# Hash products of a bucketed-attention and mixture-of-experts kernel: a second copy of queries and keys, half the columns, two diagonal blocks

## The chip, the cores and the metric

One core of one Trainium2 chip. The metric is the device time of one execution in microseconds (us); the number compared is the median of several executions of the same program.

## What is computed

Three stages follow each other; only the first is touched.

```python
q_bits = (np.einsum('bhsd,dk->bhsk', q, proj) > 0)      # 6 bits a token
k_bits = (np.einsum('bhsd,dk->bhsk', k, proj) > 0)
mask = q_bucket[:, :, :, None] == k_bucket[:, :, None, :]
scores = np.where(mask, scale * q @ k.T, -1e9)
attn = softmax(scores);  x = attn @ v                    # 2 x 8 heads, 768 tokens, 64 wide
x = moe(x)                                               # 8 experts, top 1, 512 -> 1024 -> 512
out = ((x @ w_a) * (x @ w_b)) @ w_out                    # 512 -> 1536 -> 512
```

All data are float32. The six signs of a token's product with `proj` (64 x 6) are its hash; a query sees the keys with the same hash.

## The kernel before

**Attention.** The 16 pairs of batch and head ("heads", h) run one after the other; a head has six tiles of 128 queries (t = 0 to 5), and the step counter g is 6h + t. The order of the instructions on each engine is written out by hand in the loop over g (from L740 on); waits between engines follow from the data. In step g, TensorE (PE) computes the scores of step g + 1 (`scores`, L160 and L161), then what stands in the list `early`, then the six transposes of the probabilities of step g (`tposes`, L188, two groups of three). VectorE (DVE) takes the smallest score of each row (L166) and a factor from it (L167), ScalarE (ACT) the exponential (L175). Each group of three transposes fills one of two PSUM buffers and is copied out by ACT (L192) or DVE (L194), as a table says; so the first group of a step can only be written when the copy of the first group of the step before has ended. In steps t = 1, 3 and 5 PE also multiplies the transposed probabilities of the head before with its values (`av_step`, L203), in t = 4 it makes the output of the head before that (`o_out`, L255).

**Inputs of a head.** `load` (L95) brings three DMAs on SyncE's (SP's) queue: X, queries in columns 0 to 767 and keys in 768 to 1535, where rows 64 to 127 repeat rows 0 to 63; and the values V. X has two buffers. `split_a` (L105, ACT) and `split_b` (L117 to L121, DVE and POOL) turn X into rounded parts T and remainders B of the head after next. The table `K` places them: for h > 1 the split of the queries by ACT (entry `sa`) stands in step t = 0 after the exponential.

**Hash.** `hash_mm` (L125) makes the products for head h + 1 in step t = 1 of head h (t = 0 of head 0). It is four float32 matmuls of 384 columns, two for the queries and two for the keys, each into 32 of PSUM's 128 rows (four column groups of the array). The stationary operand `pst` holds `proj`, its negative and zeros; its rows 64 to 127 are zero. `hash_codes` (L142) compares the whole block with thresholds in one DVE instruction (L144) and sends the 12 useful rows of each group by four DMAs (L149, SP's queue) into rows 64 to 75 of T. The first score matmuls of head h + 1, issued in step t = 5 of head h, read those rows (76 of 128 rows are active in L160). Head 0 takes `hash_code` (L137) instead.

**Other work on SP's queue in this stage.** 13 fills of a buffer in DRAM with zeros (L751) in heads 2 to 4, eight loads of expert weights (L506) that are issued in head 5, and in the end loads for the next stage. SP issues in order; an instruction that waits holds back everything behind it.

Of the kernel before, what the change touches and what calls it, by code (L numbers as in the profile page):

```python
# [7 lines left out]
F32 = mybir.dt.float32  # L8
F32R = mybir.dt.float32r
# [6 lines left out]
ALU = mybir.AluOpType  # L16
# [5 lines left out]
S, D, NB, NH = 768, 64, 2, 8  # L22
NT = 6
# [4 lines left out]
C_ID, C_TRI, C_THR, C_REV, C_TOK, C_IOTA, C_BASE, C_SLOT = 0, 128, 256, 258, 266, 278, 279, 287  # L28
# [6 lines left out]
def attn_moe_kernel(ctx: ExitStack, tc: tile.TileContext, xin, cst, projd, wblk, wmoe, w2in, out):  # L35
    nc = tc.nc
    PE, ACT, DVE, POOL = nc.tensor, nc.scalar, nc.vector, nc.gpsimd
# [14 lines left out]
    pst = big.tile([128, 64], F32, name="pst")  # L52
    thr = const.tile([128, 2], F32, name="thr")
# [25 lines left out]
    xp = ctx_a.enter_context(tc.tile_pool(name="xp", bufs=2))  # L79
# [4 lines left out]
    sm = ctx_a.enter_context(tc.tile_pool(name="sm", bufs=4))  # L84
# [3 lines left out]
    ps_m = ctx_a.enter_context(tc.tile_pool(name="ps_m", bufs=1, space=PSUM))  # L88

    NHD = NB * NH  # L90
    X, V, T, B, PT = {}, {}, {}, {}, {}
    st, pt_ = {}, {}
    scl, nbs, last = {}, {}, {}

    def load(h, first=()):  # L95
        X[h] = xp.tile([128, 2 * S], F32, tag="x", name="x")
        for i in range(2):
            after(nc.sync.dma_start(out=X[h][:, i * S:(i + 1) * S], in_=xin[h, :, i * S:(i + 1) * S]), first)
        V[h] = vp.tile([128, NT, D], F32, tag="v", name="v")
# [23 lines left out]
    hp_ = {}  # L123

    def hash_mm(h, order=range(4)):  # L125
        p = (ps_m if h or 2 in order else ps_a).tile([128, 512], F32, tag="m" if h or 2 in order else "a", name="m")
        for j in order:
            i = j // 2
            hp_[h, j] = p
            PE.matmul(  # L130
                p[32 * j:32 * j + 32, :384], pst[:, 32 * i:32 * i + 32], X[h][:, j * 384:(j + 1) * 384],
                start=True, stop=True, skip_group_check=True,
            )

    def hash_code(h, j):
        i, c = divmod(j, 2)
        DVE.tensor_scalar(  # L137
            out=T[h, i][64:76, c * 384:c * 384 + 384], in0=hp_[h, j][32 * j:32 * j + 12, :384],
            scalar1=thr[32 * j:32 * j + 12, 0:1], scalar2=(1.0, BIG)[i], op0=ALU.is_gt, op1=ALU.mult,
        )  # L140

    def hash_codes(h):  # L142
        c = sm.tile([128, 384], F32R, tag="code", name="code", bufs=1)
        DVE.tensor_scalar(  # L144
            out=c, in0=hp_[h, 0][:, :384], scalar1=thr[:, 0:1], scalar2=thr[:, 1:2], op0=ALU.is_gt, op1=ALU.mult
        )
        for j in range(4):
            i, k = divmod(j, 2)
            nc.sync.dma_start(  # L149
                out=T[h, i].bitcast(F32)[64:76, k * 384:k * 384 + 384], in_=c.bitcast(F32)[32 * j:32 * j + 12]  # L150
            )

    def scores(g):
        h, t = divmod(g, NT)
# [87 lines left out]
    def o_out(h, q=None):  # L242
        b, hh = divmod(h, NH)
        o, r = oT.pop((h, q)), rs.pop((h, q))
        p = ps_m.tile([128, 512], F32, tag="m", name="m")
        t0, nt = q or (0, NT)
        t = slice(b * 6 + t0, b * 6 + t0 + nt)
        lp = sm.tile([128, nt, 16], F32, tag=f"lp{nt}", name="lp", bufs=2) if hh else lg[:, t]
        if b:
            xo = x_b[:, t0:t0 + nt, hh * 64:(hh + 1) * 64]  # L250
        else:
            xf = xo = sm.tile([128, 6, 64], F32, tag="xf", name="xf", bufs=2)
        if q is None:
            for j in range(3):
                PE.matmul(p[:, j * 160:(j + 1) * 160], o[:, j * 128:(j + 1) * 128], wb[:, hh], start=True, stop=True)  # L255
            ps = p[:, :480].rearrange("p (j c n) -> p j c n", j=3, c=2)
            rr = r.rearrange("p (c j) -> p j c", c=2).unsqueeze(3)
            lo, xo, sh = lp.rearrange("p (c j) n -> p j c n", c=2), xo.rearrange("p (c j) n -> p j c n", c=2), [128, 3, 2]
        else:
            for j in range(nt):  # L260
                PE.matmul(p[:, j * 80:(j + 1) * 80], o[:, j * 128:(j + 1) * 128], wl, start=True, stop=True)
            ps = p[:, :nt * 80].rearrange("p (j n) -> p j n", j=nt)
            rr, lo, sh = r[:, :nt].unsqueeze(2), lp, [128, nt]
        DVE.tensor_tensor(out=lo, in0=ps[..., 64:], in1=rr.to_broadcast(sh + [16]), op=ALU.mult)
        DVE.tensor_tensor(out=xo, in0=ps[..., :64], in1=rr.to_broadcast(sh + [64]), op=ALU.mult)
# [371 lines left out]
    with tc.manual_schedule():  # L637
# [5 lines left out]
        POOL.memset(sums, 1e-9)  # L643
        POOL.memset(eps, 1e-9)
        nc.scalar.dma_start(out=pst[:64, 0:6], in_=projd)
        x0_in = []
        for j, q in ((2, nc.sync), (3, nc.sync), (0, nc.scalar), (1, nc.sync)):
            x0_in.append(q.dma_start(out=X[0][:, j * 384:(j + 1) * 384], in_=xin[0, :, j * 384:(j + 1) * 384]).ins)
        nc.scalar.dma_start(out=thr, in_=cst[:, C_THR:C_THR + 2])
        load(1, x0_in)  # L650
        nc.sync.dma_start(out=cs, in_=cst)
        nc.sync.dma_start(out=V[0], in_=xin[0, :, 2 * S:].rearrange("p (k d) -> p k d", d=D))
        nc.sync.dma_start(out=wb, in_=wblk[:, :640 * 2].rearrange("p (h n) -> p h n", h=NH))
        nc.sync.dma_start(out=wl, in_=wblk[:, 640 * 2:])
        DVE.tensor_copy(pst[:64, 38:44], pst[:64, 0:6])
        DVE.tensor_scalar(out=pst[:, 6:12], in0=pst[:, 0:6], scalar1=-1.0, scalar2=None, op0=ALU.mult)
        DVE.tensor_scalar(out=pst[:, 32:38], in0=pst[:, 38:44], scalar1=-1.0, scalar2=None, op0=ALU.mult)
        warm = ps_t.tile([128, 512], F32, tag="t", name="warm")
        def heat(n):
            for i in range(n):  # L660
# [49 lines left out]
        L = NHD - 1  # L710
# [29 lines left out]
        for g in range(NG):  # L740
            h, t = divmod(g, NT)
# [7 lines left out]
            if 2 * NT <= g < 2 * NT + (E * C + N) // 256:  # L749
                for i in (g - 2 * NT,):  # L750
                    nc.sync.dma_start(  # L751
                        out=xr[i * 256:(i + 1) * 256].rearrange("(p r) d -> p r d", p=128),
                        in_=zeros[0].bitcast(U32).unsqueeze(1).to_broadcast([128, 2, 512]),
# [5 lines left out]
            if g == 10 * NT + 1:  # L759
                r = router(0)  # L760
# [4 lines left out]
            early, late = [], []  # L765
            if h < L:
                if t == (1 if h else 0):
                    early.append(lambda: hash_mm(h + 1))
                if h:
                    for k in AV_AT.get(t, ()):  # L770
                        early.append(lambda k=k: av_step(h - 1, k))
                if h > 1 and t == 4:
                    (late if K["oul"] else early).append(lambda: o_out(h - 2))
            elif t < 3:
                av_step(h - 1, 2 * t)
                av_step(h - 1, 2 * t + 1)
# [15 lines left out]
            if g > 10 * NT + 1 and todo:  # L792
                f = todo.pop(0)
# [652 lines left out]
def host_inputs(q, k, v, proj, moe_w_gate, moe_w_output_gate, moe_w1, moe_w2, moe2_w_a, moe2_w_b, moe2_w_out):  # L1446
    import numpy as np

    f = np.float32
    xin = np.empty((16, 128, 1920), f)  # L1450
    qt = q.reshape(16, S, D).transpose(0, 2, 1)
    kt = k.reshape(16, S, D).transpose(0, 2, 1)
    for r in (0, 64):
        xin[:, r:r + 64, :S] = qt
        xin[:, r:r + 64, S:2 * S] = kt
    xin[:, :, 2 * S:] = v.reshape(16, NT, 128, D).transpose(0, 2, 1, 3).reshape(16, 128, NT * D)
    cst = np.zeros((128, CW), f)
    p = np.arange(128)
    cst[:, C_ID:C_ID + 128] = np.eye(128)
    cst[:, C_TRI:C_TRI + 128] = p[:, None] < p[None, :]  # L1460
    for j in range(4):
        r = 32 * j + (6 if j < 2 else 0)
        cst[r:r + 6, C_THR] = -1.2e-38
        cst[32 * j:32 * j + 32, C_THR + 1] = 1.0 if j < 2 else BIG
    cst[:, C_REV:C_REV + 8] = 8 - np.arange(8)
    cst[:, C_TOK:C_TOK + 12] = E * C + p[:, None] + 128 * np.arange(12)
# [35 lines left out]
```

## Time and profile before

| | |
|---|---|
| median of 3 executions | 722.79 us (722.61 to 722.83) |
| profiled execution, its own time | 724.47 us |
| span from its first to its last instruction | 722.7 us |
| granted TensorE clock over the span | 0.994 |
| busy: PE, DVE, ACT, POOL | 98%, 77%, 62%, 39% |

The profiled execution is 0.23% longer than the median; 1.8 us of it lie outside the span. Views of the profile give instructions in order of time, groups of instructions by source line, stretches of time with the busy share of each engine, and who waited for whom. A busy PE is not PE at its peak, since ends of matmuls are modelled; starts are recorded. A float32 matmul shows as two instructions. PEld is the weight load that goes before each matmul. Attention lasts to about 244 us.

### The profile page before, as it was taken

Reading aid. Unit: us, or ns where it says so; the run is one execution under the profiler, and the core shown is the slowest. Engines: PE = TensorE matmul, PEld = TensorE weight load, DVE = VectorE, ACT = ScalarE, POOL = GpSimd, SP = SyncE. Lnnn points to the kernel's source line nnn. Section 1 sums busy time; section 2 is a strip of 40 time slices with the busy share of each in tenths; the row PEclk is TensorE's granted clock in tenths of the full one; section 3 lists DMA queues with packets and bytes.
Section 4 is the critical chain, followed back from the end, with each engine's and each line's share of the span. In section 5 each row is a group of like instructions: output and inputs, shape, how many; then the busy total and the mean of one; then the engine's idle time right before and its main releaser. Section 6 shows DMA issues by size and latency. Waiting matters only on the chain.

```text
span 722.7 us, 13158 instructions
## 1 busy us (share of the span) xinstructions
PE 705.2 (98%) x4505; PEld 604.2 (84%) x4506; DVE 556.8 (77%) x1105; ACT 448.1 (62%) x962; POOL 283.4 (39%) x316
## 2 busy tenths in 40 slices
PE   7899999999999999999999999999999999999995
PEld 6667667667766699999999999999999999999994
DVE  5777887789777778788888878886886877777644
ACT  5787877787877637677778766575444453444320
POOL 4243334322556348845443303333322332223224
PEclk9999999999999999999999999999999999999998
DMA  7348261123212038699899741132121222122013
GB/s 241 107 164 308 85 222 59 59 65 112 104 49 64 15 128 254 174 257 213 237 288 245 229 129 59 40 107 88 59 62 55 88 76 71 55 63 59 0 51 127
DMA packets 53432, 88.01 MB, mean 122 GB/s; under 512 B 19872, under 2 KB 23280, under 8 KB 53360
## 3 DMA queue, kind: packets, MB, share of 16 engines
q1 hardware_dynamic: 50688, 80.61, 37.7%
q0 software_dynamic: 2304, 6.31, 2.3%
q8 instruction: 37, 0.61, 0.3%
q14 instruction: 35, 0.29, 0.1%
q10 hardware_dynamic: 368, 0.20, 0.1%
HBM read 69.65 MB, written 13.12 MB: 115 GB/s over the span
## 4 chain that ended last, share of the span: by engine, by line
PE 84%; issue 4%; DVE 4%; POOL 2%; DMA 2%; ACT 2%; SPq 0%; POOLq 0%; ACTq 0%; DVEq 0%
PE tp L188 9%; PE av L203 8%; PE y L1033 6%; PE s L161 4%; PE s L160 4%; PE h L995 4%; PE h L994 4%; PE h L993 3%; PE aba L1270 3%; PE aba L1272 3%; PE abb L1270 3%; PE aba L1271 3%; PE abb L1272 3%; PE abb L1271 3%; PE y L1034 3%
## 5 line engine op out<-in xcount | busy, mean ns | idle before, releaser
L166 DVE TENSOR_REDUCE mm<-s 128x1 f32<-128x768 f32 x96 | 91.1, 949 | 26.7 <-PE s L161 25.8
L175 ACT ACTIVATE p<-s,sb 128x768 f32<-128x768 f32 x96 | 95.0, 989 | 21.2 <-DVE sb L167 20.4
L188 PEld LDWEIGHTS tp<-cs,p 128*128 128x128 f32 x576 | 64.9, 141 | 37.9 <-ACT p L175 24.4
L188 PE MATMUL tp<-cs,p 128*128 128x128 f32 x576 | 82.7, 280 | 6.4 <-DMA cs<-cst 2.9
L516 DVE TENSOR_TENSOR wl<-wr,wh 128x512 fp32r<-128x512 f32 x125 | 83.2, 705 | 4.9 <-ACT wh L515 1.1
L192 ACT ACTIVATE pt<-tp 128x384 f32<-128x384 f32 x143 | 65.1, 487 | 34.7 <-PE tp L188 34.7
L964 POOL TENSOR_TENSOR pc<-t,pc 128x256 fp32r<-128x256 f32 x38 | 33.1, 873 | 134.8 <-ACT pc L963 119.2
L1033 PE MATMUL y<-hl,wh 128*128 128x448 f32 x224 | 75.0, 378 | 0.6 <-DVE hl L1007 0.5
L515 ACT ACTIVATE wh<-wr 128x512 fp32r<-128x512 f32 x128 | 73.7, 624 | 1.3 <-DMA wr<-wmoe 1.2
L160 PE MATMUL s<-tk,tq 76*128 76x384 f32 x192 | 73.7, 384 | 0.3 <-DVE tq L137 0.3
L994 PE MATMUL h<-xl,wh 128*128 128x224 f32 x256 | 70.3, 275 | 0.5 <-DVE xl L450 0.3
L995 PE MATMUL h<-xh,wl 128*128 128x224 f32 x256 | 70.6, 276 | 0.0
L993 PE MATMUL h<-xh,wh 128*128 128x224 f32 x256 | 70.3, 275 | 0.2 <-ACT xh L449 0.2
L203 PE MATMUL av<-pt,v 128*64 128x384 f32 x360 | 68.0, 499 | 0.2 <-DVE r L238 0.2
L161 PE MATMUL s<-bk,bq 128*128 128x384 f32 x192 | 65.6, 342 | 0.0
L1034 PE MATMUL y<-hl,wl 128*128 128x224 f32 x224 | 59.5, 266 | 0.0
L964 POOL TENSOR_TENSOR pc<-s,pc 128x256 fp32r<-128x256 f32 x44 | 38.0, 875 | 33.0 <-ACT pc L963 32.0
L118 POOL CAST bq<-tq 64x768 fp32r<-64x768 f32 x15 | 21.2, 1414 | 74.8 <-ACT tq L105 47.4
L1160 ACT ACTIVATE gh<-p 128x384 fp32r<-128x384 f32 x21 | 11.0, 526 | 63.2 <-DVE p L1289 63.2
L993 PEld LDWEIGHTS h<-xh,wh 128*128 128x128 f32 x256 | 48.9, 191 | 1.5 <-ACT xh L449 0.4
L994 PEld LDWEIGHTS h<-xl,wh 128*128 128x128 f32 x256 | 49.1, 192 | 1.0 <-DVE xl L450 0.5
L203 PEld LDWEIGHTS av<-pt,v 128*64 128x64 f32 x360 | 21.9, 136 | 32.8 <-issue 24.5
(264 smaller groups left out, 2002.6 us busy)
## 6 DMA issues: line engine op xcount, KB each, us to landing
wr<-wmoe SPq DMA_DIRECT2D x128, 256.0 KB
r<-w2in SPq DMA_DIRECT2D x36, 512.0 KB
x<-xin SPq DMA_DIRECT2D x30, 384.0 KB
xr<-zero SPq DMA_DIRECT2D x13, 512.0 KB
v<-xin SPq DMA_DIRECT2D x16, 192.0 KB
wb<-wblk SPq DMA_DIRECT2D x1, 640.0 KB
x<-xin SPq DMA_DIRECT2D x3, 192.0 KB
tq<-code SPq DMA_DIRECT2D x30, 18.0 KB
```

The lines of the kernel that those rows point to most:

```text
L160: PE.matmul(p[:, c, :384], T[h, 0][:76, qs], T[h, 1][:76, sl], start=True, stop=False)
L161: PE.matmul(p[:, c, :384], B[h, 0][:, qs], B[h, 1][:, sl], start=False, stop=True)
L166: DVE.tensor_reduce(out=m[:, 1:2], in_=st[g][:, :, :384], axis=AX.XY, op=ALU.min)
L175: ACT.activation(p.rearrange("p (c n) -> p c n", c=2), st.pop(g)[:, :, :384], ACTF.Exp, scale=scl.pop(g), bias=nbs.pop(g), accum_out=sums[ ...
L188: PE.transpose(ps[:, j * 128:(j + 1) * 128], pt_[g][:, k * 128:(k + 1) * 128], ident)
L203: PE.matmul(av[h][c * 64:(c + 1) * 64, :384], v, PT[h][:, k, c * 384:(c + 1) * 384], start=(k == 0), stop=(k == NT - 1), skip_group_check= ...
L516: eng.tensor_tensor(out=l, in0=r, in1=h.bitcast(F32), op=ALU.subtract)
L993: PE.matmul(ps, wh, xh, start=first, stop=False)
L994: PE.matmul(ps, wh, xl, start=False, stop=False)
L995: PE.matmul(ps, wl, xh, start=False, stop=last)
L1033: PE.matmul(p, wh[:, w], hl, start=(f == 0), stop=False, skip_group_check=True)
L1034: PE.matmul(p[:, 0], wl[:, w], hl[:, 0], start=False, stop=(f == 7), skip_group_check=True)
```

## The change

The host adds a second copy of queries and keys, `XT`, of 768 columns: columns 0 to 383 are for the queries, 384 to 767 for the keys; rows 0 to 63 hold tokens 0 to 383, rows 64 to 127 tokens 384 to 767. `pst` gets a second block of `proj` and its negative in rows 64 to 127, 12 columns further on. For heads 2 to 15 `hash_halves` then makes the same products with matmuls of 192 columns (head 0 and 1 keep `hash_mm`). The block of codes is 192 wide and each group has 24 useful rows, so eight DMAs of half the length bring the codes into T. `XT` has one buffer; its load for head h + 2 is issued after the codes of head h + 1. To make room, the buffer `xf` of the outputs of batch 0 is single instead of double, and the code block of head 1 shares buffers with `o`. At the start `proj` is loaded twice and its copies are made by six small DVE instructions instead of three.

```diff
+    def load_halves(h):
+        XT[h] = xp.tile([128, S], F32, tag="xt", name="xt", bufs=1)
+        nc.sync.dma_start(out=XT[h], in_=xin[h, :, 2 * S + NT * D:])
...
+    def hash_halves(h):
+        p = ps_m.tile([128, 512], F32, tag="m", name="m")
+        for j in range(4):
+            i = j // 2
+            hp_[h, j] = p
+            PE.matmul(
+                p[32 * j:32 * j + 32, :192], pst[:, 32 * i:32 * i + 32], XT[h][:, j * 192:(j + 1) * 192],
+                start=True, stop=True, skip_group_check=True,
+            )
...
     def hash_codes(h):
-        c = sm.tile([128, 384], F32R, tag="code", name="code", bufs=1)
+        n = 192 if h > 1 else 384
+        c = sm.tile([128, n], F32R, tag="code" if h > 1 else "o", name="code", bufs=1 if h > 1 else 2)
         DVE.tensor_scalar(
-            out=c, in0=hp_[h, 0][:, :384], scalar1=thr[:, 0:1], scalar2=thr[:, 1:2], op0=ALU.is_gt, op1=ALU.mult
+            out=c, in0=hp_[h, 0][:, :n], scalar1=thr[:, 0:1], scalar2=thr[:, 1:2], op0=ALU.is_gt, op1=ALU.mult
         )
         for j in range(4):
             i, k = divmod(j, 2)
-            nc.sync.dma_start(
-                out=T[h, i].bitcast(F32)[64:76, k * 384:k * 384 + 384], in_=c.bitcast(F32)[32 * j:32 * j + 12]
-            )
+            for r in range(384 // n):
+                at = r * 384 + k * n
+                nc.sync.dma_start(
+                    out=T[h, i].bitcast(F32)[64:76, at:at + n],
+                    in_=c.bitcast(F32)[32 * j + 12 * r:32 * j + 12 * r + 12],
+                )
...
-            xf = xo = sm.tile([128, 6, 64], F32, tag="xf", name="xf", bufs=2)
+            xf = xo = sm.tile([128, 6, 64], F32, tag="xf", name="xf", bufs=1)
...
         nc.scalar.dma_start(out=pst[:64, 0:6], in_=projd)
+        nc.scalar.dma_start(out=pst[64:, 12:18], in_=projd)
...
-        DVE.tensor_copy(pst[:64, 38:44], pst[:64, 0:6])
-        DVE.tensor_scalar(out=pst[:, 6:12], in0=pst[:, 0:6], scalar1=-1.0, scalar2=None, op0=ALU.mult)
-        DVE.tensor_scalar(out=pst[:, 32:38], in0=pst[:, 38:44], scalar1=-1.0, scalar2=None, op0=ALU.mult)
+        for r, c in ((0, 0), (64, 12)):
+            p = pst[r:r + 64]
+            DVE.tensor_copy(p[:, c + 38:c + 44], p[:, c:c + 6])
+            for to in (6, 32):
+                DVE.tensor_scalar(
+                    out=p[:, c + to:c + to + 6], in0=p[:, c:c + 6], scalar1=-1.0, scalar2=None, op0=ALU.mult
+                )
...
         load(2)
+        load_halves(2)
...
-                    early.append(lambda: hash_mm(h + 1))
+                    early.append(lambda: (hash_halves if h else hash_mm)(h + 1))
...
                 if h < L and (t, pos) == (1, 0):
                     hash_codes(h + 1)
+                    if 0 < h < L - 1:
+                        load_halves(h + 2)
```

Two places where the order of instructions shows the change. On PE in step t = 1 of a head, the hash (`m`) stands between the scores (`s`) and the values' product (`av`); before:

```order
L160 MATMUL s<-tk,tq 128x384
L161 MATMUL s<-bk,bq 128x384
L130 MATMUL m<-x,pst 32x384 x4
L203 MATMUL av<-pt,v 64x384 x4
L188 MATMUL tp<-cs,p 128x128 x6
```

and with the change (lines are those of the changed file; L179 and L180 are the scores, L222 the values' product, L207 the transposes):

```order
L179 MATMUL s<-tk,tq 128x384
L180 MATMUL s<-bk,bq 128x384
L145 MATMUL m<-xt,pst 32x192 x4
L222 MATMUL av<-pt,v 64x384 x4
L207 MATMUL tp<-cs,p 128x128 x6
```

Nothing moved on PE; the hash has half the columns and another operand. On SP's queue, in a head without zero fills or weight loads (`x`, `v` the inputs of the head three further on, `tq`, `tk` the parts T of queries and keys; the names in brackets are what the instruction waits for: DMAHW a DMA eight DMAs back), before:

```order
L98 DMA x_1353<-xin 128x768 [waits DVE_49,DMAHW7_49,PE_49,Pool_49]
L98 DMA x_1353<-xin 128x768 [waits DMAHW0_49]
L100 DMA v_1356<-xin 128x384 [waits DMAHW1_49]
L149 DMA tq_1160<-code_1378 12x384 [waits DMAHW2_49,DVE_49]
L149 DMA tq_1160<-code_1378 12x384 [waits DMAHW3_49]
L149 DMA tk_1226<-code_1378 12x384 [waits DMAHW4_49]
L149 DMA tk_1226<-code_1378 12x384 [waits DMAHW5_49]
L98 DMA x_1528<-xin 128x768 [waits DVE_49,DMAHW6_49,PE_49,Pool_49]
```

and with the change:

```order
L98 DMA x_1389<-xin 128x768 [waits DMAHW2_49,DVE_49,Pool_49]
L98 DMA x_1389<-xin 128x768 [waits DMAHW3_49]
L100 DMA v_1392<-xin 128x384 [waits DMAHW4_49,PE_49]
L167 DMA tq_1190<-code_1414 12x192 [waits DMAHW5_49,DVE_49]
L167 DMA tq_1190<-code_1414 12x192 [waits DMAHW6_49]
L167 DMA tq_1190<-code_1414 12x192 [waits DMAHW7_49]
L167 DMA tq_1190<-code_1414 12x192 [waits DMAHW0_49]
L167 DMA tk_1262<-code_1414 12x192 [waits DMAHW1_49]
L167 DMA tk_1262<-code_1414 12x192 [waits DMAHW2_49]
L167 DMA tk_1262<-code_1414 12x192 [waits DMAHW3_49]
L167 DMA tk_1262<-code_1414 12x192 [waits DMAHW4_49]
L105 DMA xt_1424<-xin 128x768 [waits DMAHW5_49,PE_49]
```

Four issues became eight, the load of `XT` stands behind them, and the load of X no longer waits for PE (the hash read X; now only the splits do). The load of V waits for PE, which frees its buffer at the end of the head before.

## Rows read from the trace of the kernel before

**Rows 1.** The page, part 1: busy time, share of the span, instructions.

```profile
PE 705.2 (98%) x4505; PEld 604.2 (84%) x4506; DVE 556.8 (77%) x1105; ACT 448.1 (62%) x962; POOL 283.4 (39%) x316
```

**Rows 2.** Stretch between hashes: length, busy PE, PEld, DVE, ACT, POOL (instructions), clock, DMA share.

```profile
116.40:130.96 14.56, 14.56 (x100) 10.26 (x99) 11.43 (x23) 11.40 (x23) 5.41 (x5) 1.00 0.22 74
```

**Rows 3.** Timeline, PE around one hash: start, length, instruction, count.

```profile
87.29 0.85 PE L130 MATMUL m<-x,pst 128*32 128x384 f32 x8
...
88.07 1.51 PE L203 MATMUL av<-pt,v 128*64 128x384 f32 x8
```

**Rows 4.** Stretches of that hash, its instructions alone: PE busy (running), PEld, clock.

```profile
87.28:87.60 0.32, 0.31 (x4) 0.16 (x8) 1.00 0.00 0
87.60:87.66 0.06, 0.06 (x8) 0.00 (x0) 1.00 0.00 0
```

**Rows 5.** Timeline, DVE, ACT and PE around that hash, from the step before it.

```profile
85.00 0.56 DVE L194 COPY pt<-tp 128x384 f32<-128x384 f32 x1 [0.70 <-PE tp L188]
...
86.24 0.92 DVE L166 TENSOR_REDUCE mm<-s 128x1 f32<-128x768 f32 x1
...
87.52 0.99 ACT L175 ACTIVATE p<-s,sb 128x768 f32<-128x768 f32 x1 [0.27 <-DVE sb L167]
...
88.50 0.83 ACT L105 ACTIVATE tq<-x 128x768 fp32r<-128x768 f32 x1
...
89.23 0.98 ACT L175 ACTIVATE p<-s,sb 128x768 f32<-128x768 f32 x1
...
89.51 0.87 PE L188 MATMUL tp<-cs,p 128*128 128x128 f32 x6
...
90.20 0.49 ACT L192 ACTIVATE pt<-tp 128x384 f32<-128x384 f32 x1
...
90.76 0.75 PEld L188 LDWEIGHTS tp<-cs,p 128*128 128x128 f32 x6
90.94 0.82 PE L188 MATMUL tp<-cs,p 128*128 128x128 f32 x6
```

**Rows 6.** Timeline, the codes of that head: DVE, SP's queue, and the scores that read them.

```profile
88.69 0.68 DVE L144 TENSOR_SCALAR code<-m,thr 128x384 fp32r<-128x384 f32 x1
...
89.64 1.53 SPq L149 DMA_DIRECT2D tq<-code  x2
...
96.90 0.19 PEld L160 LDWEIGHTS s<-tk,tq 76*128 76x128 f32 x1
```

**Rows 7.** Groups by line, attention: count, busy us, mean ns, idle before.

```profile
L265 DVE TENSOR_TENSOR xf<-m,r 128x384 f32<-128x384 f32 x8 | 4.3, 541 | 0.0
...
L264 DVE TENSOR_TENSOR lp<-m,r 128x96 f32<-128x96 f32 x13 | 3.2, 246 | 1.0 <-PE m L255 1.0
```

**Rows 8.** Timeline of SP's queue, the codes of head 15: start, length, DMA.

```profile
220.78 0.68 DVE L144 TENSOR_SCALAR code<-m,thr 128x384 fp32r<-128x384 f32 x1
...
221.52 1.48 SPq L149 DMA_DIRECT2D tq<-code  x2
...
223.10 1.48 SPq L149 DMA_DIRECT2D tk<-code  x2
```

**Rows 9.** Stretches behind the last issue of Rows 8; last two columns DMA share, GB/s.

```profile
225.10:225.60 0.50, 0.47 (x4) 0.00 (x0) 0.50 (x1) 0.50 (x2) 0.50 (x1) 1.00 0.17 37
225.60:225.80 0.20, 0.00 (x0) 0.00 (x0) 0.20 (x1) 0.20 (x3) 0.08 (x1) 1.00 0.00 0
```

**Rows 10.** Timeline of SP's queue in head 3, among the zero fills.

```profile
61.11 2.02 SPq L149 DMA_DIRECT2D tq<-code  x2
```

**Rows 11.** Timeline of the start: ACT's queue, first transposes.

```profile
1.10 0.56 ACTq L645 DMA_DIRECT2D pst<-projd  x1
...
4.00 0.16 DVE L655 COPY pst<-pst 64x6 f32<-64x6 f32 x1 [3.89 <-DMA pst<-projd]
...
14.03 0.95 PE L188 MATMUL tp<-cs,p 128*128 128x128 f32 x6 [2.92 <-DMA cs<-cst]
```

**Rows 12.** Who waited for whom, SP's queue in attention: us, times, longest.

```profile
SPq L98 <- PE m L130: 96.3, 12, 10.3
```

More of the change, by code (lines that the diff above doesn't have):

```diff
@@ L90, in attn_moe_kernel @@
     NHD = NB * NH
-    X, V, T, B, PT = {}, {}, {}, {}, {}
+    X, XT, V, T, B, PT = {}, {}, {}, {}, {}, {}
     st, pt_ = {}, {}
@@ L99, in load @@
         V[h] = vp.tile([128, NT, D], F32, tag="v", name="v")
-        nc.sync.dma_start(out=V[h], in_=xin[h, :, 2 * S:].rearrange("p (k d) -> p k d", d=D))
+        nc.sync.dma_start(out=V[h], in_=xin[h, :, 2 * S:2 * S + NT * D].rearrange("p (k d) -> p k d", d=D))
+    def load_halves(h):
+        XT[h] = xp.tile([128, S], F32, tag="xt", name="xt", bufs=1)
+        nc.sync.dma_start(out=XT[h], in_=xin[h, :, 2 * S + NT * D:])
     def split_a(h, i, lo=0, n=S):
@@ L651, in attn_moe_kernel @@
         nc.sync.dma_start(out=cs, in_=cst)
-        nc.sync.dma_start(out=V[0], in_=xin[0, :, 2 * S:].rearrange("p (k d) -> p k d", d=D))
+        nc.sync.dma_start(out=V[0], in_=xin[0, :, 2 * S:2 * S + NT * D].rearrange("p (k d) -> p k d", d=D))
         nc.sync.dma_start(out=wb, in_=wblk[:, :640 * 2].rearrange("p (h n) -> p h n", h=NH))
         nc.sync.dma_start(out=wl, in_=wblk[:, 640 * 2:])
-        DVE.tensor_copy(pst[:64, 38:44], pst[:64, 0:6])
-        DVE.tensor_scalar(out=pst[:, 6:12], in0=pst[:, 0:6], scalar1=-1.0, scalar2=None, op0=ALU.mult)
-        DVE.tensor_scalar(out=pst[:, 32:38], in0=pst[:, 38:44], scalar1=-1.0, scalar2=None, op0=ALU.mult)
+        for r, c in ((0, 0), (64, 12)):
[5 more added lines that the diff above has]
+                )
         warm = ps_t.tile([128, 512], F32, tag="t", name="warm")
@@ L1449, in host_inputs @@
     f = np.float32
-    xin = np.empty((16, 128, 1920), f)
+    xin = np.empty((16, 128, 2 * S + NT * D + S), f)
     qt = q.reshape(16, S, D).transpose(0, 2, 1)
@@ L1455, in host_inputs @@
         xin[:, r:r + 64, S:2 * S] = kt
-    xin[:, :, 2 * S:] = v.reshape(16, NT, 128, D).transpose(0, 2, 1, 3).reshape(16, 128, NT * D)
+        for i, x in enumerate((qt, kt)):
+            at = 2 * S + NT * D + i * 384
+            xin[:, r:r + 64, at:at + 384] = x[:, :, 6 * r:6 * r + 384]
+    xin[:, :, 2 * S:2 * S + NT * D] = v.reshape(16, NT, 128, D).transpose(0, 2, 1, 3).reshape(16, 128, NT * D)
     cst = np.zeros((128, CW), f)
@@ L1461, in host_inputs @@
     for j in range(4):
-        r = 32 * j + (6 if j < 2 else 0)
-        cst[r:r + 6, C_THR] = -1.2e-38
+        for r in (0, 12):
+            r += 32 * j + (6 if j < 2 else 0)
+            cst[r:r + 6, C_THR] = -1.2e-38
         cst[32 * j:32 * j + 32, C_THR + 1] = 1.0 if j < 2 else BIG
```

## Prediction
> **What bounds the kernel now.** First the busy shares: PE is at 98% [rows 1], so time goes where PE's does. The change touches only the hash in attention, so next the stretches from one hash to the next: a head lasts 14.56 us, PE is busy all of it at full clock, DVE and ACT for 11.4 us each [rows 2]. Busy is not yet bound, so third the timeline of one head, for who releases PE at each step. The reader is to see there two things: how long PE is held by the hash, and how little time lies between the other engines' results and PE's use of them. Fourth the queue that carries the codes (SP), because the change doubles its issues.
>
> **The hash on PE.** It starts at 87.29 and the next work on PE, the values' product, at 88.07 [rows 3]: 0.78 us. Its eight instructions run as two rounds of four: four are under way until 87.60, and within the next 0.06 us the second four start [rows 4]. A round so lasts 0.31 to 0.37 us for 384 columns; I take 0.32, which leaves 0.14 us that belongs to loading weights and to changing between forms, and stays. With 192 columns a round takes 0.16: the hash falls to 0.46, by **0.32 us**. 14 heads have the new hash (h = 1 to 14, for heads 2 to 15), so at most 14 x 0.32 = 4.5 us. If the rounds were held by something other than columns the gain would be 0; the recorded starts speak for columns.
>
> **Who is late next.** Behind the hash PE does the values' product, six transposes, four score matmuls and then the first transposes of step t = 2. Those write the PSUM buffer that ACT empties: the copy starts at 90.20 and lasts 0.49, so it ends at 90.69, and PE's weight load for these transposes starts at 90.76 [rows 5]. That is 0.07 us of room against 0.32 won. Could ACT be earlier? Its chain begins before the hash: DVE's copy at 85.00, released by the transposes of step t = 5, DVE's score minimum 86.24, then ACT, released by DVE and from there without a gap: exponential 87.52, split of the queries 88.50, exponential 89.23, copy 90.20 [rows 5]. Nothing in it reads the hash. So PE will wait there for ACT. It does not lose all: now the load at 90.76 is queued ahead, its matmuls start at 90.94 and the six end at 91.76; when such a group starts on an empty PE, it ends 0.87 after its start (89.51) [rows 5]. A start at 90.74 gives 91.61. The head gains **0.14 us** instead of 0.32. This holds where ACT's split of the queries stands in that chain, heads 2 to 13: 12 x 0.14 = 1.7. Head 1 has the split elsewhere and head 14 has none: 2 x 0.32 = 0.6. Together **2.3 us gained**; bounds 0 and 4.5.
>
> **The codes.** The block's DVE instruction takes 0.68 [rows 6]; from 96 to 384 columns an operation on PSUM grows from 246 to 541 ns [rows 7], about 1 ns a column, so 192 columns less make it 0.48. DVE starts it at 88.69 for reasons that lie before the hash, so the codes are ready at 89.17. On a free queue the first DMA follows 0.06 us behind (220.78 + 0.68, then 221.52) [rows 8]; now it is 0.27 (88.69 + 0.68, then 89.64 [rows 6]), since SP is then still issuing X and V, which waited for PE's hash (96.3 us in 12 waits [rows 12]). That wait goes, X and V are issued in the head before, and SP is free. An issue takes 0.72 to 0.79 with its gap (two in 1.58: 221.52 to 223.10; the last two end 1.48 after the first of them starts [rows 8]). I take 0.775 for each, as nothing in it depended on the length. The eighth is then issued at 89.23 + 7 x 0.775 = 94.66. Bytes stop moving 1.2 to 1.7 us after the last issue (223.10 + 0.77 = 223.87; the stretch to 225.60 still has traffic, the next none) [rows 9]; with word to PE I take 2.0, where the load of `proj` at the start, from DRAM, took 2.9 (issue at 1.10, DVE's first use at 4.00 [rows 11]), and the row nearest in kind is that of the codes. So the last codes are there at 96.66. The scores' second pair, the first to need them, has its weight load at 96.90 [rows 6], 96.76 after a gain of 0.14. **Margin 0.1 us, price 0**; what stands behind a late code is PE itself, with all 14 heads.
>
> The Trainium skill, "DMA: Bandwidth & Descriptors", section "Issuing engines are not separate DMA queues", says that the sequencer's time to start a DMA is usually small beside the transfer. By that rule the eight issues would cost next to nothing and no code could be late. The rows here show the opposite: 0.77 of issue against about 1.3 of the rest, and issue alone makes 5.4 of the 7.5 us from codes to scores.
>
> **Heads with a full queue.** In head 3 the first two code issues took 2.02 instead of 1.53 [rows 10], behind X, V and a zero fill. The change puts another 384 KB into the same queues (`XT`, 5.5 MB in all) ahead of them. With a margin of 0.1 I count 0.3 us each for heads 3 and 4: **+0.6**; bounds 0 and 2 (twice the whole 2.0 issue, in two heads). Elsewhere `XT` is hidden: it is loaded a head, 14 us, before its use, and DMA is busy for 0.22 of such a stretch [rows 2].
>
> **Start.** The second load of `proj` on ACT's queue, 0.56 and a gap [rows 11], stands ahead of a piece of head 0's X and of ACT's first work. The loads of head 1 wait for all pieces, and the table `cs` behind them ends PE's idle time at 14.03 [rows 11]. The delay is between 0 (the piece is held by the transfer) and 0.6: I take **+0.4**. Three more small DVE instructions there end before ACT's first output does.
>
> **Single `xf`.** POOL reads it as soon as DVE has written it and the next write is a head, 14.5 us [rows 2], later: 0; uncovered, it would cost DVE one write, 0.54 [rows 7], for each of 8 heads.
>
> **Sum.** -2.3 + 0.6 + 0.4 = -1.3 us on the profiled execution: 724.47 to 723.2. The median is 1.68 lower, so **721.5 us** (-0.18%). The later stages are only shifted.
>
> **Rivals.**
>
> *The whole gain shows.* ACT's chain would have to move with PE; it does not, by its rows. But the 0.07 us of room is small against what I read from modelled ends, and a little slack in the split or in the copy's start would give it back. 14 x 0.32 = 4.5 less 1.0 of the start and the full queues: -3.5, 719.3 us. Then the deadline for the codes moves to 96.58 and they, not ACT, are the next limit.
>
> *Codes too late (slower).* At each head's fifth step, PE would wait for the eighth DMA. Against it: the margin. For it: the margin is 0.1 us, of a path of eight issues. At 0.82 an issue, 0.03 above the mean of the rows, the last codes come at 89.23 + 5.74 + 2.0 = 96.97, and with 0.05 for PE to start, 0.12 later than now: 14 x 0.12 = 1.7, with 1.0 from start and full queues +2.7, **725.5 us**. It decides from an arrival of 96.9 on: there the head's gain is gone. Each further 0.1 costs 1.4.
>
> *Nothing is left.* The round does not shrink in proportion, or the codes come just at the time at which they are needed now: the hash gains 0, start and full queues are lower than taken: 722.8.
>
> **How the numbers follow.** Forecast 50%, its own range -2.6 to +0.3 us (720.2 to 723.1): the gain of 2.3 with start and full queues between nothing (and 0.3 more gain) and their bounds of 0.6 and 2. Whole gain 20%, codes late 16%, nothing left 14%. About 0.2%, 1.45 us, is what can be told from no change. Faster by more than that (below 721.34): 45% of the forecast's cases, 0.22, and the whole gain, 0.20: 0.42. Slower: most of the late codes, 0.14, and 0.03 of nothing left: 0.17. Same: the remaining 0.41. The range leaves out the lower half of the whole gain and the upper half of the late codes: 718.9 to 725.0.
>
> **What would show it.** In the profile after: a hash from first start to the values' product of 0.46; the first transposes of step t = 2 starting right when ACT's copy ends, with PE idle before them; heads of 14.4 us; code DMAs in eight issues of 0.77, the first 0.06 behind DVE; no wait of the scores for a DMA except in heads 3 and 4; X issued some 8 us earlier. A head of 14.2 us would say that ACT's chain was no limit; waits of L179 on a code DMA in every head would say that the margin was misjudged; first transposes at 14.0 would say that the start cost nothing.

## The result, and the profile after

| | before | after |
|---|---|---|
| median | 722.81 us | 727.67 us |
| ratio, 95% interval | | 1.0070 (1.0052 to 1.0087) |
| profiled execution, its own time | 724.47 us | 727.04 us |
| from the hash for head 3 (in head 2) to the first product of the next stage | 43.62 to 261.90: 218.28 us | 41.21 to 264.62: 223.41 us |

The change costs 4.9 us, outside the range and on the other side of the forecast. The last line of the table leaves out the start, which differs from execution to execution (last section): there it is 5.1 us.

First the busy shares after, which answer to [rows 1]: PE does the same work in a longer span.

```profile
PE 705.2 (97%) x4505; PEld 602.7 (83%) x4506; DVE 553.2 (76%) x1108; ACT 447.5 (62%) x962; POOL 282.1 (39%) x316
```

Then stretches from one hash to the next, as [rows 2] (length; busy PE, PEld, DVE, ACT, POOL; clock; DMA share, GB/s), each from the hash in one head to that in the next; they begin in heads 2, 3, 9, 10 and 13:

```profile
41.21:55.57 14.36, 14.36 (x99) 10.14 (x99) 10.92 (x23) 11.38 (x23) 5.12 (x5) 1.00 0.66 228
55.57:74.33 18.76, 16.46 (x99) 11.16 (x99) 11.21 (x23) 11.49 (x23) 5.40 (x5) 0.91 0.80 284
146.41:160.81 14.40, 14.40 (x99) 10.18 (x98) 11.12 (x24) 11.38 (x23) 5.01 (x4) 1.00 0.30 102
160.81:176.74 15.93, 15.34 (x108) 10.36 (x107) 13.67 (x30) 11.61 (x23) 3.47 (x3) 1.00 0.27 93
206.04:220.48 14.44, 14.44 (x100) 10.13 (x99) 11.22 (x24) 11.40 (x24) 5.13 (x5) 1.00 0.13 38
```

Most heads do what was forecast: 14.4 us where they took 14.55. The one that begins in head 3 takes 18.76, with PE idle for 2.3 us of it and a lower clock; the one that begins in head 10 takes 15.93.

An ordinary head, as [rows 3 to 5] showed it:

```profile
117.58 0.53 PE L145 MATMUL m<-xt,pst 128*32 128x192 f32 x8
118.05 1.51 PE L222 MATMUL av<-pt,v 128*64 128x384 f32 x8
...
118.75 0.16 DVE L186 SCALAR_TENSOR_TENSOR sb<-mm 128x2 f32<-128x2 f32 x1
...
119.18 0.48 DVE L160 TENSOR_SCALAR code<-m,thr 128x192 fp32r<-128x192 f32 x1 [0.27 <-issue]
...
120.49 0.48 ACT L211 ACTIVATE pt<-tp 128x384 f32<-128x384 f32 x1
...
121.03 0.87 PE L207 MATMUL tp<-cs,p 128*128 128x128 f32 x6
```

The hash takes 0.47. ACT's copy ends at 120.97 and PE's transposes start 0.06 later. The codes go out on SP in eight issues from 119.69 on, the last ending at 125.78 (122.79 + 2.99), and the second pair of scores loads its weights at 127.06 and waits for nothing:

```profile
119.69 3.06 SPq L167 DMA_DIRECT2D tq<-code  x4
122.79 2.99 SPq L167 DMA_DIRECT2D tk<-code  x4
...
127.06 0.19 PEld L179 LDWEIGHTS s<-tk,tq 76*128 76x128 f32 x1
```

Where the time went, by who waited for whom on PE up to 256 us (total, times, longest):

```profile
PE s L179 <- DMA tk<-code: 2.7, 4, 2.1
...
PE m L274 <- DVE o L253: 0.7, 1, 0.7
PE tp L207 <- DVE pt L213: 0.6, 2, 0.3
```

So the codes are late in a few places, above all in head 3. SP's queue there:

```profile
49.62 0.45 SPq L105 DMA_DIRECT2D xt<-xin  x1
50.12 5.00 SPq L776 DMA_DIRECT2D xr<-zero  x5
55.23 2.58 SPq L98 DMA_DIRECT2D x<-xin  x2
57.91 0.69 SPq L100 DMA_DIRECT2D v<-xin  x1
58.66 0.55 SPq L776 DMA_DIRECT2D xr<-zero  x1
59.31 4.26 SPq L167 DMA_DIRECT2D tq<-code  x4
63.62 2.99 SPq L167 DMA_DIRECT2D tk<-code  x4
66.72 0.44 SPq L105 DMA_DIRECT2D xt<-xin  x1
```

SP issues without a pause: from 49.62 to 66.72 one round, 17.1 us, where a head has 14.4. DVE had the codes ready at 57.65; their first issue comes at 59.31. PE, and then its clock (stretches as above):

```profile
67.06 0.42 PE L179 MATMUL s<-tk,tq 76*128 76x384 f32 x1 [2.05 <-DMA tk<-code]
...
67.90 0.41 PE L179 MATMUL s<-tk,tq 76*128 76x384 f32 x1 [0.25 <-DMA tk<-code]
68.15 0.33 PE L180 MATMUL s<-bk,bq 128*128 128x384 f32 x1
68.42 2.19 PE L222 MATMUL av<-pt,v 128*64 128x384 f32 x8
70.54 1.54 PE L207 MATMUL tp<-cs,p 128*128 128x128 f32 x6
```

```profile
66.00:68.00 2.00, 0.69 (x3) 0.43 (x4) 0.00 (x0) 0.56 (x2) 0.47 (x1) 1.00 0.21 31
69.00:72.00 3.00, 3.00 (x13) 1.70 (x10) 1.16 (x4) 1.08 (x2) 0.00 (x0) 0.52 1.04 405
72.00:74.00 2.00, 2.00 (x14) 1.96 (x14) 1.69 (x5) 1.08 (x3) 0.00 (x0) 0.87 1.05 406
```

PE stood idle for 2 us, and behind that the granted clock was 0.52, near the lower of its two levels (1.2 GHz), for some 3 us: the values' product takes 2.19 there and 1.51 elsewhere.

### The profile page after: what moved, and what is told of

The parts are those of the page before. It is cut to its first block, busy times and chain, and to the rows that moved or that the text cites. A ratio compares the mean times of both kernels' runs of the same rounds, so it can differ in the third digit from the quotient of the medians.

```text
span 725.3 us, 13288 instructions
## 1 busy us (share of the span) xinstructions
PE 705.2 (97%) x4505; PEld 602.7 (83%) x4506; DVE 553.2 (76%) x1108; ACT 447.5 (62%) x962; POOL 282.1 (39%) x316
## 4 chain that ended last, share of the span: by engine, by line
PE 79%; issue 5%; DVE 4%; POOL 4%; ACT 2%; DMA 2%; SPq 2%; ACTq 0%; POOLq 0%; DVEq 0%
PE tp L207 7%; PE av L222 7%; PE y L1060 6%; PE h L1022 4%; PE h L1021 4%; PE h L1020 4%; PE s L179 3%; PE s L180 3%; PE aba L1297 3%; PE aba L1299 3%; PE aba L1298 3%; PE abb L1297 3%; PE abb L1299 3%; PE abb L1298 3%; PE y L1061 3%
## 5 line engine op out<-in xcount | busy, mean ns | idle before, releaser
L207 PEld LDWEIGHTS tp<-cs,p 128*128 128x128 f32 x576 | 63.8, 141 | 40.0 <-ACT p L194 28.1
L207 PE MATMUL tp<-cs,p 128*128 128x128 f32 x576 | 83.4, 281 | 5.0 <-ACT p L194 4.1
L179 PE MATMUL s<-tk,tq 76*128 76x384 f32 x192 | 73.6, 383 | 3.4 <-DMA tk<-code 2.7
L222 PE MATMUL av<-pt,v 128*64 128x384 f32 x360 | 68.7, 503 | 0.2 <-DVE r L257 0.2
L180 PE MATMUL s<-bk,bq 128*128 128x384 f32 x192 | 65.2, 340 | 0.0
L1022 PEld LDWEIGHTS h<-xh,wl 128*128 128x128 f32 x256 | 49.2, 192 | 0.0
```

The lines of the kernel that those rows point to most:

```text
L179: PE.matmul(p[:, c, :384], T[h, 0][:76, qs], T[h, 1][:76, sl], start=True, stop=False)
L180: PE.matmul(p[:, c, :384], B[h, 0][:, qs], B[h, 1][:, sl], start=False, stop=True)
L207: PE.transpose(ps[:, j * 128:(j + 1) * 128], pt_[g][:, k * 128:(k + 1) * 128], ident)
L222: PE.matmul(av[h][c * 64:(c + 1) * 64, :384], v, PT[h][:, k, c * 384:(c + 1) * 384], start=(k == 0), stop=(k == NT - 1), skip_group_check= ...
L1022: PE.matmul(ps, wl, xh, start=False, stop=last)
```

## Experiments

The theory: the matmuls gain what was forecast, and the eight issues take more than that back, in four places (heads 3, 10, 14 and the end of attention). The rivals: the bytes of `XT`; X sent ahead of the codes; the single buffers or the start. The last column runs, as above, from the hash for head 3 to the first product of the next stage, by their starts in the trace of each kernel.

| kernel | median us | ratio to before (95%) | stretch us |
|---|---|---|---|
| before | 722.5 to 723.4 | 1 | 218.28 |
| after | 727.67 | 1.0070 (1.0052 to 1.0087) | 223.41 |
| cols_only | | | 41.97 to 258.09: 216.12 |
| half_codes | | | 40.92 to 257.04: 216.12 |
| spread | 724.51 | 1.0023 (1.0012 to 1.0034) | 41.71 to 262.02: 220.31 |
| load_behind | 726.34 | 1.0048 (1.0026 to 1.0070) | 40.89 to 263.83: 222.94 |
| eight_before | 734.30 | 1.0163 (1.0146 to 1.0179) | 45.91 to 272.75: 226.84 |
| dummy_before | 726.55 | 1.0064 (1.0050 to 1.0078) | 43.83 to 264.30: 220.47 |
| dummy_sbuf | 732.19 | 1.0125 (1.0099 to 1.0152) | 45.24 to 270.29: 225.05 |
| gather_first | 726.09 | 1.0051 (1.0038 to 1.0064) | 41.36 to 263.38: 222.02 |
| pool_half | 731.20 | 1.0116 (1.0098 to 1.0134) | 42.62 to 265.09: 222.47 |
| via_dram | 719.48 | 0.9953 (0.9938 to 0.9968) | 41.68 to 257.99: 216.31 |
| via_dram_order | 719.54 | 0.9958 (0.9946 to 0.9971) | 40.90 to 256.49: 215.59 |
| via_dram_order_sa | 717.56 | 0.9933 (0.9919 to 0.9946) | 41.42 to 255.43: 214.01 |

**The hash alone, and all but four issues.** cols_only, on the kernel before (the comparison and the DMAs cut to `n` columns likewise):

```diff
+            n = 192 if h > 1 else 384
...
-                p[32 * j:32 * j + 32, :384], pst[:, 32 * i:32 * i + 32], X[h][:, j * 384:(j + 1) * 384],
+                p[32 * j:32 * j + 32, :n], pst[:, 32 * i:32 * i + 32], X[h][:, j * 384:j * 384 + n],
```

> The kernel before, with the hash of heads 2 to 15 made from the first 192 columns of each group alone (the other half of the tokens is left out), one DVE comparison of 192 columns, and four code DMAs as before; no second copy, no more issues. Theory 'ACT is next': 12 heads gain 0.14 us and two 0.32, together 2.3: 720.5 us against 722.8, heads of 14.41. Rival 'the hash is not priced by columns': 722.8, hash still 0.78. Rival 'nothing else is in the way': 14 x 0.32 = 4.5, 718.3, heads of 14.23.

half_codes, on the changed kernel:

```diff
-            for r in range(384 // n):
+            for r in range(1):
```

> The changed kernel with four of its eight code DMAs (the codes of the second half of the tokens are left out); second copy and its load stay. Theory 'codes late in four places': what the eight issues cost goes, that is 2.2 us and the clock loss of 1.6 in heads 3 and 4, 0.7 in head 10, 0.4 in head 14, and the gather of expert rows, queued behind the codes in head 14, comes 3 us earlier (0.9): about 722 us. Rival 'the bytes of XT fill the queues': the issues matter little, 726 or more, with head 4 still over 16 us.

Values change with the codes in both, so that at the end the program's loop for rows beyond an expert's capacity runs; their totals (1510 and 1710 us) say nothing, and attention alone is read. cols_only takes 216.12 where before takes 218.28: 2.16 less (of the forecast 2.3, 2.0 lie in this stretch: 12 x 0.14 and 0.32), with heads of 14.42:

```profile
113.95:128.37 14.42, 14.42 (x100) 10.19 (x99) 10.98 (x23) 11.39 (x23) 5.40 (x5) 1.00 0.20 72
```

half_codes takes 216.12 too. It has `XT`, its load, the single `xf`, the second load of `proj`. So none of these costs anything behind the start, and the four DMAs more in each head are the whole loss of 7.3 us (223.41 - 216.12). In the heads with fills DMA is busier than in the changed kernel, 0.91, and nothing is late:

```profile
55.26:69.69 14.43, 14.43 (x100) 10.19 (x99) 11.00 (x23) 11.39 (x23) 5.42 (x5) 1.00 0.91 316
```

The same stretch on SP: counted from the hash, X goes out 3.2 us earlier than after (51.69 against 55.26; after, 55.23 against 55.57), and the codes as soon as DVE has them (57.14).

```profile
51.69 2.50 SPq L98 DMA_DIRECT2D x<-xin  x2
54.29 0.43 SPq L100 DMA_DIRECT2D v<-xin  x1
54.76 0.55 SPq L776 DMA_DIRECT2D xr<-zero  x1
57.16 1.76 SPq L167 DMA_DIRECT2D tq<-code  x2
58.97 1.47 SPq L167 DMA_DIRECT2D tk<-code  x2
```

**Order on SP.** spread, on the changed kernel:

```diff
-            if 2 * NT <= g < 2 * NT + (E * C + N) // 256:
-                for i in (g - 2 * NT,):
+            if g % 2 == 0 and 8 <= g < 8 + 2 * ((E * C + N) // 256):
+                for i in ((g - 8) // 2,):
```

> The changed kernel with the 13 zero fills put in every second step from step 8 to 32 in place of every step from 12 to 24. Theory 'codes behind a full queue in heads 3 and 4': SP never issues more than three fills in a row, the codes of head 4 go out at once, heads 3 and 4 take 14.4 us and the clock stays at 1.00: 3.8 us less, 723.9. Rival 'eight issues are too many in any head': codes still arrive too late, 726 or more.

load_behind:

```diff
-            if t == 1 and h + 3 < NHD:
-                load(h + 3)
...
                     if 0 < h < L - 1:
                         load_halves(h + 2)
+                    if h + 3 < NHD:
+                        load(h + 3)
```

> The changed kernel with the loads of X and V issued behind the code DMAs in place of ahead of them; fills stay. Theory 'X goes out too early, into a queue full of fills, and holds the codes': the first code issue of head 4 follows DVE at once, the arrival is 2 us earlier, and most of 3.8 us is back: 724 to 725. Rival 'the fills themselves hold the codes': each of the first code issues still takes over 1 us and the codes stay late by over 1 us: 726 to 727.5.

spread gains 3.1 us of the stretch: the 18.76 becomes 14.80 (56.12 to 70.91). It does not reach the 3.8 forecast, since the weight loads of head 6, no longer held up behind fills, now stand ahead of X and of the codes made in head 6 (eight loads, 95.28 to 100.31; DVE ready at 102.25, first code at 103.45), and the stretch behind takes 15.50. load_behind gains 0.5 us, and its stretch from head 3 to 4 still takes 18.53: its rival was right, X ahead of the codes is not what holds them. SP's issues add up to too much, in whatever order; the first four codes take 4.20 us there, from 58.56 on, where an ordinary head has 3.06.

**The issues alone.** eight_before, on the kernel before:

```diff
+            for r in (0, 192):
+                nc.sync.dma_start(
+                    out=T[h, i].bitcast(F32)[64:76, k * 384 + r:k * 384 + r + 192],
+                    in_=c.bitcast(F32)[32 * j:32 * j + 12, r:r + 192],
+                )
```

> The kernel before, with each of its four code DMAs cut into two of 192 columns; hash, loads and the rest stay. Theory 'the eight issues are the whole loss': head 4's codes 2 us late and the clock lower behind it, codes late in heads 11 and 15 and the gather in head 14 later by 3 us: 5 to 6 us longer, 728 to 729, with a hash of 0.78. Rival 'XT, its traffic and the single buffers cost it': 723.

dummy_before and dummy_sbuf, also on the kernel before, with a line ahead of each code DMA (`waste` in DRAM, or 4 x 64 columns of SBUF):

```diff
+            nc.sync.dma_start(out=waste[j], in_=cs[64:76, :192])
```

```diff
+            nc.sync.dma_start(out=waste[64:76, j, :], in_=cs[64:76, :64])
```

> The kernel before, with a DMA of the same size that carries a constant to a spare place ahead of each of its four code DMAs: SP issues eight, but DVE's comparison waits for four. Theory 'two costs, SP's issue time and DVE's waits for the block's DMAs': heads without fills keep 14.55 us (the eight halves had 14.96), heads 4 and 5 and the end of attention still lose: 726 to 728. Rival 'issue time alone': as with the eight halves, 734.

> As the run with the constants, but the constant goes to spare rows of SBUF (12 rows of 64 columns), since the ones to DRAM took 0.5 us of SP a piece and the codes 0.75: now all eight issues should take about 0.75. Theory 'two costs': heads without fills 14.55 to 14.6 us with the last code 5.7 us behind DVE, just in time; heads with fills lose as with the eight halves less what DVE's waits cost, 728 to 731. Rival 'eight equal issues alone make heads of 14.96': 734.

eight_before loses 11.4 us, twice what was expected, 8.6 of it in the stretch: besides the late codes, every ordinary head takes 14.94 to 14.98 in place of 14.55. The loss begins on DVE. The comparison writes the block that the DMAs of the head before read, and now waits for eight of them; the timeline shows 0.27 idle between DVE's `sb` and the comparison, where before shows 0.08 (103.01 + 0.16 to 103.25):

```profile
109.62 0.16 DVE L169 SCALAR_TENSOR_TENSOR sb<-mm 128x2 f32<-128x2 f32 x1
110.05 0.68 DVE L144 TENSOR_SCALAR code<-m,thr 128x384 fp32r<-128x384 f32 x1 [0.27 <-DMA wr<-wmoe]
110.64 1.58 DVE L117 SCALAR_TENSOR_TENSOR bq<-x,tq 64x768 fp32r<-64x768 f32 x1
112.15 0.54 DVE L196 COPY pt<-tp 128x384 f32<-128x384 f32 x1
```

The delay of 0.2 grows behind it. The product for `bq` takes 1.58 here and 0.95 in before, and the row of POOL's cast of the same tile says why. First before, then eight_before:

```profile
103.92 0.95 DVE L117 SCALAR_TENSOR_TENSOR bq<-x,tq 64x768 fp32r<-64x768 f32 x1
104.00 1.56 POOL L118 CAST bq<-tq 64x768 fp32r<-64x768 f32 x1 [5.49 <-issue]
```

```profile
110.59 0.82 POOL L118 CAST bq<-tq 64x768 fp32r<-64x768 f32 x1 [5.29 <-issue]
```

The one that starts first takes its short time (0.95 on DVE, 0.82 on POOL), and the other ends 1.63 to 1.64 us after that start, as if it ran behind it. In before DVE starts 0.08 ahead; here POOL does, by 0.05, and DVE takes 0.63 more. PE's transposes of that step then wait 0.16 for DVE's copy.

dummy_sbuf has the same eight issues of 0.71 to 0.76 but a comparison that waits for four DMAs: it starts 0.08 behind `sb`, and ordinary heads take 14.59 to 14.62 (139.11 to 153.73, for one), as the theory said, but for one of 14.94, where the comparison comes 0.43 behind `sb`, POOL's cast is first and `bq` takes 1.42; the head with fills behind head 3 takes 18.64 (60.92 to 79.56). Its 732.19 lies above the range of the theory, 728 to 731, and below the rival's 734. So there are two costs, shown apart: SP's issue time, which makes heads with fills late, and the block's waits on DVE. In dummy_before the constants to DRAM took SP 0.4 to 0.6 each, not 0.75, and less was lost; that is why dummy_sbuf followed.

After, the same gap of 0.27 stands in every ordinary head (above, 118.75 + 0.16 to 119.18; 0.08 in half_codes, where four DMAs read the block); there it is paid by the comparison, which is 0.2 shorter with 192 columns, and DVE stays ahead of POOL (119.65, 119.74). In head 10 the comparison is later still:

```profile
162.77 0.48 DVE L160 TENSOR_SCALAR code<-m,thr 128x192 fp32r<-128x192 f32 x1 [0.62 <-issue]
```

POOL's cast is again ahead (162.97), `bq` takes DVE 1.45, PE's transposes then wait 0.3 for DVE's copy, and the scores 0.2 for the codes. What made 0.62 out of 0.27 there the profile does not show. It need not be the eight waits: the head of 14.94 in dummy_sbuf has the same 0.35 more (0.43 in place of 0.08) with four. Nor does it show why one code issue there (among the four from 166.37 on) takes 1.35 us.

**The end of attention.** gather_first:

```diff
-            (0, 0): [split_behind(0)],
-            (0, 1): [x0_load, behind(lambda: late_planes(0)), lambda: late_planes(1)],
+            (0, 0): [split_behind(0), x0_load],
+            (0, 1): [behind(lambda: late_planes(0)), lambda: late_planes(1)],
```

> The changed kernel with the gather of expert rows in head 14 issued a step earlier, ahead of the codes of head 15. Theory 'POOL waits for that gather, and head 15 for POOL': the time from head 15's first scores to the last values' product goes back from 24.9 to 23.6, 1.3 us less: 726.4. Rival 'head 15 is slower for another reason': 727.7.

After, POOL waits for that gather, which SP issues at 229.75, behind the eight codes (before: 224.90):

```profile
232.54 1.45 POOL L433 COPY x<-x0q 128x512 uint16<-128x512 uint16 x2 [4.05 <-DMA x0q<-xr]
```

With the gather ahead of the codes the same copy starts without a wait:

```profile
228.14 1.43 POOL L433 COPY x<-x0q 128x512 uint16<-128x512 uint16 x2
```

From the last hash to the next stage the times are 42.54 in half_codes, 44.14 after (220.48 to 264.62) and 43.20 here (220.18 to 263.38): 0.94 of 1.6 us is the gather. The scores' wait for codes in head 14 is still there (0.1). The median, 726.09, is near the 726.4 expected for 1.3 us less; the stretch is shorter by 1.39, of which the gather is the 0.94.

The rest lies in heads 3 and 4, where this kernel is the changed one, and it says something about the clock. PE waits for the codes as long as after (2.07 and 0.25), but the granted clock stays at 1.00. The stretches that begin in heads 3 and 4:

```profile
55.72:72.91 17.19, 14.88 (x99) 10.16 (x98) 10.97 (x23) 11.39 (x23) 5.40 (x5) 1.00 0.76 269
72.91:88.36 15.45, 14.86 (x99) 10.16 (x98) 10.96 (x23) 11.39 (x23) 5.40 (x5) 1.00 0.69 240
```

Together they take 32.64, after 33.19 (18.76 and 14.43). At full clock SP is still late in the second: its first code goes out 1.05 behind DVE (74.99, 76.04), and PE idles 0.6 more; after, with PE slower, 0.02 behind (76.41, 76.43).

**Another queue.** pool_half:

```diff
-                nc.sync.dma_start(
+                (POOL if r else nc.sync).dma_start(
```

> The changed kernel with four of the eight code DMAs issued by POOL in place of SP. Theory 'SP's issue time': SP is as free as with four, POOL's issues take about 1.0 us each (as its scatters in head 12) and end 4 us behind DVE, arrival at 6 to 7: 721 to 724. Rival 'POOL's own work is next': its copies and splits come 4 us later in every head and hold the scores: 728 or more.

The rival was right. POOL needs only 0.5 us an issue, and heads 3 and 4 lose nothing to the fills. But ordinary heads take 14.57, and two later ones 16.45 and 16.19 (159.46, 175.91, 192.10), with PE waiting 4.5 us for ACT's copies over attention; 4.4 more are lost behind attention; their cause was not traced.

**Fewer issues.** via_dram, on the changed kernel (with `proj`'s second block in columns 16 to 21, and the second copy's columns in the order of T):

```diff
+            nc.sync.dma_start(out=code_d[h % 2], in_=c.bitcast(F32))
...
+    def code_rows(h):
+        for i in range(2):
+            nc.sync.dma_start(
+                out=T[h, i].bitcast(F32)[64:76].rearrange("p (b n) -> p b n", b=4),
+                in_=code_d[h % 2][64 * i:64 * i + 64].rearrange("(b z) n -> z b n", b=4)[:12],
+            )
```

> The changed kernel with three issues for the codes in place of eight: the whole block goes to DRAM in one DMA, and one DMA each brings the queries' and the keys' codes back in the rows of T (the second block of proj 4 columns further on, the second copy in another order of tokens, so that the rows form one pattern). Theory 'issues': arrival at 0.1 + 0.6 + 1.9 + 2 x 0.75 + 1.9 = 6.0 us behind DVE on a free queue, under 7.2: heads of 14.41, gather earlier, 720.5 to 722.5, the upper end if two hops behind the fills are late in heads 3 and 4. Rival 'each hop takes 2.9, as the load of proj did': 8.0, late in every head, 728 or more.

via_dram_order puts `load(h + 3)` behind `code_rows(h + 1)`, and:

```diff
+            if 1 < t < 5 and h and 3 * (h - 1) + t - 2 < (E * C + N) // 256:
+                for i in (3 * (h - 1) + t - 2,):
...
-            if g == 6 * NT:
+            if g == 6 * NT + 2:
```

> As via_dram, and on SP's queue X and V stand behind the codes, the fills three a head in steps 2 to 4 of heads 1 to 5, the eight weight loads two steps later. Theory: the queues are empty when the codes are sent, no head waits for them: 720.5. Rival 'DMA traffic was no matter once the issues are few': the same as via_dram within 0.5.

via_dram_order_sa, one entry of the table `K`:

```diff
-'sa': ((0, 2), (2, 2))
+'sa': ((0, 1), (2, 2))
```

> As via_dram_order, with ACT's split of the queries ahead of the second copy-out of step t = 0 in place of behind the exponential. Theory 'ACT's chain is what keeps 0.18 of each 0.32 us': heads of 14.23 in place of 14.41, 12 x 0.18 = 2.2 less than via_dram_order, 718.3. Rival 'DVE or the codes are next at the same place': no change, 720.5; or the split now delays an exponential: above that.

via_dram is 3.4 us faster than before, and 1.0 below the range expected (720.5 to 722.5). SP's codes in a head of via_dram_order:

```profile
114.66 0.33 SPq L165 DMA_DIRECT2D code_d<-code  x1
115.08 0.38 SPq L106 DMA_DIRECT2D xt<-xin  x1
116.33 0.32 SPq L175 DMA_DIRECT2D tq<-code_d  x1
116.74 0.32 SPq L175 DMA_DIRECT2D tk<-code_d  x1
```

Three issues of 0.33 each, less than half of what a code DMA within SBUF takes, and the way to DRAM is done 1.67 after its issue. The order gains 0.7 us of the stretch (those that begin in heads 3 and 4 took 14.81 and 14.82 in via_dram and 14.41 here), the medians show no difference, as its rival said. The moved split makes heads of 14.24, as the theory of ACT's chain said:

```profile
112.59:126.83 14.24, 14.24 (x100) 10.25 (x99) 11.02 (x23) 11.27 (x24) 4.68 (x5) 1.00 0.38 124
```

That is 1.6 us in the stretch, for 2.2 expected (the three from head 10 to head 13 gain nothing between them), and the fastest of all: 717.56, 5.3 us under the kernel before.

## Why the prediction was wrong

- **The hash** (0.46 instead of 0.78): right, 0.47.
- **Who is late next** (ACT, 0.14 a head): right. Heads fell by 0.14, the transposes start 0.06 behind ACT's copy, and with ACT's split out of that chain the other 0.18 comes too. cols_only measures 2.16 where 2.0 was forecast.
- **The codes in an ordinary head** (margin 0.1, price 0): right. The issues took 0.76 and no ordinary head waits. That DVE would have them 0.2 earlier was wrong: the comparison is 0.2 shorter and starts 0.2 later, since it now waits for eight DMAs of the head before. That wait is one that the change adds and the prediction did not list.
- **Heads with a full queue** (+0.6, bounds 0 and 2): this is the step that failed. I priced two slow issues, and held that SP would be free once X no longer waits for PE. In heads 2 to 4 SP is not waiting, it is issuing: behind full queues a fill takes 1.0 on average and a piece of X 1.3. The sum over a head, 17.1 us against 14.4, was never made. The trace of before had most of its prices: five fills 4.88, two pieces of X up to 1.39, the first two codes 2.02 [rows 10]. With them eight codes, V, the sixth fill and `XT` make about 14.7, an estimate that already fills the head; that X would go out behind fills, at 1.3 a piece, it did not show. The stretch costs 18.76 - 14.43 = 4.33 us.
- **The clock**: not priced at all. Of the 4.33, 2.30 are waits for codes. From the values' product to the next hash PE takes 5.91 us (68.42 to 74.33), in half_codes 4.33 (65.36 to 69.69): 1.58 for the stretch at the lower level; 0.45 was not traced. But gather_first keeps the full clock behind the same wait and loses most of that in the next head instead, so by these two executions the lower level made 0.55 of the 4.35 that both heads cost, and what brought it in one execution and not in the other is open.
- **"The later stages are only shifted"**: right, 460.7 us from their first product to the end, before 460.8. But the sum put two places of attention at nothing that are not. The stretch that begins in head 10 loses 1.3 (15.93; half_codes 14.62), and the end 1.6, of which 0.94 is the gather behind the codes on SP. What is queued behind the codes was listed for the heads with fills, not there.
- **`XT`, single `xf`**: 0 was right. **Start** (+0.4): lies within what starts differ by.

The sum by what was measured: -2.16, then 4.33 + 1.31 + 1.60 = 7.24 back, which makes 5.08 of the 5.13 us; this divides the difference up and is no second measurement of it. The rival "codes too late" had the mechanism and its sign, but as 0.12 us in every head; the wait is 0 in most and 2.3 in one, and with what follows from it that one costs 3.8 to 4.4.

On the rule that I weighed (the Trainium skill, "DMA: Bandwidth & Descriptors", section "Issuing engines are not separate DMA queues": the time to start a DMA is usually small beside the transfer), the traces stay with the rows: 0.75 an issue for 9 KB within SBUF, and four DMAs more a head, of 3 KB each, that nothing reads, cost dummy_sbuf 6.8 us of the stretch (225.05 - 218.28).

## What to carry to other kernels

Sum the issue time of a DMA queue over one period and compare it with the period, at the prices that its issues have while the queues are full; twice the DMAs can be harmless in most heads and cost more than the gain in one. A late transfer costs its wait and then more: on a full queue the next transfers are late too, and in some executions the clock falls behind the wait. And count who waits for the DMAs that you add: the next writer of their source waits for each of them, and a small delay can change which of two engines goes first.

## What was not expected of the hardware

- Away from the fills, a DMA of 12 rows within SBUF takes SP 0.71 to 0.76 us in most cases, with 64, 192 or 384 columns alike; one of 128 rows from SBUF to DRAM 0.33, and one that brings 12 rows of 768 columns back 0.32. Two hops with three issues were cheaper than eight direct ones.
- Waiting for eight DMAs in place of four cost DVE 0.2 us each time, though all of them had long landed.
- DVE's product and POOL's cast for `bq` start within 0.1 us of each other, and the later one ends 1.63 to 1.64 us after the first start, for lengths of 0.95 and 0.82; in eight_before a delay on DVE changed which of them was held, and heads of 14.55 became 14.98.
- The start differs between executions: PE's wait for `cs` was 2.92 in the profile of before [rows 11], 2.8 in dummy_before, 2.1 in pool_half, 1.4 in via_dram, 1.3 in spread and absent in the others. Behind it, in the profile of before, the clock is at the lower level for some 3 us, as in head 4 after; so it is in dummy_before and pool_half. A term that is costed on one execution's start is costed on chance.
